# Adding the second half of an output in memory with GpSimd's transfers instead of on VectorE

## The chip, the cores and the metric

The kernel runs on one core of a Trainium2 chip. Its time is the device time of one execution in microseconds (us). Before the change three runs took 1242.47, 1244.1 and 1243.73 us; the median is 1243.73 us.

## The reference, cut to what matters

Three stages follow each other on 8 batches (`x` is 8 x 8 x 512 x 64, `state` 8 x 8 x 32 x 64):

```
xread, sread = state attention of x and state        # 8 x 544 rows, 512 columns
x   = (max(xa @ w_in, 0) ** 2) @ w_out               # 4352 rows; 512 -> 2048 -> 512
out = (((x @ w1) * (x @ w2)) @ w3) @ w_out2          # 512 -> 1024 -> 1024 -> 512, float32
```

Only the last line touches the change. The kernel multiplies `w3 @ w_out2` once into one 1024 x 512 matrix (`w34`), so that the last line is a product of 4352 x 1024 activations `c` with `w34`. The 1024 inner rows are summed in two halves of 512.

## The kernel before, in words

Every float32 product is made of three passes (high times high, low times high, high times low), so one logical product is three MATMUL instructions of 128 x 128 by 512 columns.

The 4352 output rows are nine pieces: `c` = 0 to 7 are the 512 token rows of each batch (four tiles of 128 rows each), and `c` = 8 (called `B` in the code) holds the 8 x 32 state rows (two tiles). So there are 34 output tiles of 128 x 512 float32, 256 KB each.

The last stage goes over all pieces twice, in two sweeps (loop at L952). Sweep `s` = 0 computes the first 512 columns of `c` and their part of the output, sweep 1 the other 512 columns and the rest of the output. Within a sweep the state piece comes first (`ab9`, then two output tiles), then four pairs of batches: (3,4), (5,6), (7,2), (0,1) in sweep 0 and the same in reverse in sweep 1. A pair is four calls of `quad` (42 matmuls each; L825 to L862) and then eight output tiles.

- `out_tile` (L904) is one output tile: 12 matmuls into a PSUM bank called `po` (tag `h`, two banks). In sweep 0 ScalarE copies the bank to an SBUF tile `o` (L916) and SyncE stores it to a scratch tensor `oscr` (L917). In sweep 1 VectorE adds the bank and the scratch tile that was loaded again (`opart`), into `o` (L919), and SyncE stores `o` into the output (L923, or L928 for the state rows, four stores of 32 rows a tile).
- `o` has the tag `yo` with two buffers: the tile after next can be written only when the transfer out of the buffer has landed.
- `load_o` (L899) loads `oscr` again. Its buffers are shared: `pt` with the loads of `load_pair` (L785), `s1` and `s2` with two of the temporaries that `quad` keeps (L836).
- `load_pair` (L778) loads the next pair's activations, 2 MB, on SyncE's queue; where a piece had been written in parts, the parts are added by GpSimd (L787). `make_pair` (L791) turns them into split tiles on ScalarE (L84) and VectorE (L85, L804) while the output tiles run.

The order on each engine is laid down by a scheduler when the kernel is built; the program's order is only its starting point. So the trace shows matmuls of the next pair's `quad` between output tiles.

Of the kernel before, what the change touches and what calls it, by code (L numbers as in the profile page):

```python
# [8 lines left out]
F32 = mybir.dt.float32  # L9
# [4 lines left out]
ALU = mybir.AluOpType  # L14
# [6 lines left out]
def kernel(  # L21
# [17 lines left out]
    nc = tc.nc  # L39
    B, H, S, D = x.shape  # L40
    NS = state.shape[2]
    DM = H * D
    DF = w_in.shape[1]
    D1 = w1.shape[1]
    T = S + NS
    P = 128
    G = 2
    HG = H // G
    J = S // P
# [9 lines left out]
    def f32(ap):  # L59
        return ap.bitcast(F32)  # L60
# [4 lines left out]
    dram = ctx.enter_context(tc.tile_pool(name="dram", bufs=1, space=DRAM))  # L65
# [8 lines left out]
    def bank_h(name):  # L74
        return psum.tile([P, 512], F32, tag="h", bufs=2, name=name)
# [476 lines left out]
    xp, sc, s2, s1a, s1b, at, a2t, sr, srt = att_steps(0)  # L552
# [74 lines left out]
    for b in range(BLK, B):  # L627
# [5 lines left out]
        for g in range(G):  # L633
            i = (b - 2) * NF + 12 + g
# [103 lines left out]
    bp = None  # L738

    def load_w(s):  # L740
        raw = []
        for kt in range(2):
            t = wpool.tile([P, 4, 512], F32, tag="wi1", bufs=2, name="wraw")
            for n, (i, k) in enumerate(((0, kt), (0, 2 + kt), (1, kt), (1, 2 + kt))):
                nc.sync.dma_start(t[:, n], w12_s[i][k][:, s, :])
            raw.append(t)
        return raw
# [30 lines left out]
    def load_pair(c0, c1):  # L778
        raw = []
        for kt in range(2):  # L780
            t = wpool.tile([P, 4, 512], F32, tag="wi1", bufs=2, name="yraw")
            for n, (c, d) in enumerate(((c0, kt), (c1, kt), (c0, 2 + kt), (c1, 2 + kt))):
                nc.sync.dma_start(t[:, n], y_scr[c][0][:, d, :])
                for part in y_scr[c][1:]:
                    p = bp.tile([P, 512], F32, tag="pt", bufs=2, name="yp")  # L785
                    nc.sync.dma_start(p, part[:, d, :])
                    nc.gpsimd.tensor_tensor(out=t[:, n], in0=t[:, n], in1=p, op=ALU.add)  # L787
            raw.append(t)
        return raw
# [35 lines left out]
    def quad(c0, c1, m):  # L825
        def product(ps, w, v, first=True, last=True):
            for kt in range(2):
                for k, (wi, vi) in enumerate(PASSES):
                    nc.tensor.matmul(  # L829
                        ps, W[w, kt][:, wi, m * P:(m + 1) * P], Y[v, kt][:, vi, :],  # L830
                        start=(first and kt == 0 and k == 0), stop=(last and kt == 1 and k == 2),
                        skip_group_check=True,
                    )

        def kept(i, ps):
            t = bp.tile([P, 512], F32, tag=f"s{i}", bufs=1 + (i == 0), name=f"s{i}")  # L836
            nc.scalar.copy(t, ps)  # L837
            return t

        def plus(t, ps):  # L840
            nc.vector.tensor_tensor(out=t, in0=ps, in1=t, op=ALU.add)  # L841

        A, D, E, C = bank_m("qa"), bank_y(m % 2, "qd"), bank_y(2, "qe"), bank_y(3, "qc")
        product(A, "A11", "B11", last=False)
        p1 = kept(0, A)
        product(D, "S1", "T1", last=False)
        p5 = kept(1, D)
        product(E, "A12", "B21")
        plus(p1, E)
        product(A, "S2", "T2", first=False, last=False)  # L850
        u2 = kept(2, A)
        product(D, "S4", "B22", first=False)
        plus(u2, D)
        product(C, "A22", "T4")
        product(A, "S3", "T3", first=False)
        u3 = kept(3, A)
        plus(p5, A)
        nc.vector.tensor_tensor(out=u2, in0=u2, in1=p5, op=ALU.mult)  # L858
        to_c(c1, m, u2, 512)
        plus(u3, C)  # L860
        nc.vector.tensor_tensor(out=p1, in0=p1, in1=u3, op=ALU.mult)
        return to_c(c0, m, p1, 512)  # L862
# [9 lines left out]
    def make9(raw):  # L872
        for d in range(ND):
            t = bp.tile([P, 2, 512], F32R, tag="c", bufs=2 * QM, name="y9q")
            split(t[:, HI, :NT9], t[:, LO, :NT9], raw[d // 2][:, d % 2])
            Y[B, d] = t

    def ab9(m):
        pss = [bank_y(2 * i + m % 2, "ab") for i in range(2)]
        for i in range(2):  # L880
            for d in range(ND):
                w = W[f"A{i + 1}{d // 2 + 1}", d % 2]
                for k, (wi, vi) in enumerate(PASSES):
                    nc.tensor.matmul(  # L884
                        pss[i][:, :NT9], w[:, wi, m * P:(m + 1) * P], Y[B, d][:, vi, :NT9],
                        start=(d == 0 and k == 0), stop=(d == ND - 1 and k == 2),
                    )
        a = bp.tile([P, 512], F32, tag="s0", bufs=2, name="a")
        nc.scalar.copy(a[:, :NT9], pss[0][:, :NT9])
        nc.vector.tensor_tensor(out=a[:, :NT9], in0=pss[1][:, :NT9], in1=a[:, :NT9], op=ALU.mult)  # L890
        to_c(B, m, a[:, :NT9], NT9)

    def n_out(c):
        return (512 if c < B else NT9) // P

    o_scr = {(c, t): dram.tile([P, DM], F32, name=f"oscr{c}_{t}") for c in range(B + 1) for t in range(n_out(c))}
    o_in = {}

    def load_o(c, t):  # L899
        tag = ("pt", "pt", "s1", "s2")[t]  # L900
        o_in[c, t] = bp.tile([P, DM], F32, tag=tag, bufs=2 if tag == "pt" else 1, name="opart")
        nc.sync.dma_start(o_in[c, t], o_scr[c, t])

    def out_tile(c, t, s):  # L904
        ps = bank_h("po")
        for m in range(QM):
            v, kk = c_t[c, m], s * QM + m
            w = w34_t[kk // 2][:, kk % 2]
            for k, (vi, wi) in enumerate(PASSES):
                nc.tensor.matmul(  # L910
                    ps, v[:, vi, t * P:(t + 1) * P], w[:, wi, :],
                    start=(m == 0 and k == 0), stop=(m == QM - 1 and k == 2),
                )
        o = pa.tile([P, DM], F32, tag="yo", bufs=2, name="o")
        if s == 0:
            nc.scalar.copy(o, ps)  # L916
            nc.sync.dma_start(o_scr[c, t], o)  # L917
            return
        nc.vector.tensor_tensor(out=o, in0=ps, in1=o_in.pop((c, t)), op=ALU.add)  # L919
        if c < B:  # L920
            rows_t = "(p j) e -> j p e" if c < BLK else "(j p) e -> j p e"
            dst = out[c * T:c * T + S, :].rearrange(rows_t, j=J)[t]
            nc.sync.dma_start(dst, o)  # L923
        else:
            nb = P // NS
            for i in range(nb):
                r0 = (t * nb + i) * T + S
                nc.sync.dma_start(out[r0:r0 + NS, :], o[i * NS:(i + 1) * NS, :])  # L928


    rows = list(range(N1 // 2, N1)) + list(range(N1 // 2))
# [13 lines left out]
    bp = ctx.enter_context(tc.tile_pool(name="bp", bufs=1, reuse_waits="tile"))  # L945
# [6 lines left out]
    for s, todo in enumerate((pairs, pairs[::-1])):  # L952
        if s == 1:
            make9(raw9)
            for t in range(n_out(B)):
                load_o(B, t)
        for m in range(QM):
            ab9(m)
        for t in range(n_out(B)):
            out_tile(B, t, s)  # L960
        for i, (c0, c1) in enumerate(todo):
            for m in range(QM):
                last = quad(c0, c1, m)
                if m == 0 and i + 1 < len(todo):
                    raw = load_pair(*todo[i + 1])
                if m == 1 and i + 1 == len(todo) and s == 0:
                    raw = load_w(1)
            outs = [(c, t) for c in (c0, c1) for t in range(n_out(c))]
            if s == 1:
                for o in outs[:3]:  # L970
                    load_o(*o)
            for n, (c, t) in enumerate(outs):
                if s == 1 and n + 3 < len(outs):
                    load_o(*outs[n + 3])
                out_tile(c, t, s)
                with tc.issue_after(last.ins):
                    if n == 0 and i + 1 < len(todo):
                        make_pair(raw)
                    if n == 0 and i + 1 == len(todo) and s == 0:
                        raw9 = load9()  # L980
                        make_w(raw)
            if s == 0 and i + 1 == len(todo):
                for j in range(N1 // 4):
                    w34_t[N1 // 4 + j] = wpool.tile([P, 2, 2, DM], F32R, tag="wi0", bufs=2, name="w34b")
                    nc.sync.dma_start(f32(w34_t[N1 // 4 + j]), w34_s[j])
# [29 lines left out]
```

## Time and profile before

| what | value |
| --- | --- |
| median of three runs | 1243.73 us |
| profiled execution, its own time | 1244.7 us |
| its span in the trace | 1242.7 us |
| granted TensorE clock, mean | 0.995 of full speed |
| TensorE busy | 1226.2 us (99%) |
| VectorE busy | 780.8 us (63%) |
| ScalarE busy | 623.9 us (50%) |
| GpSimd busy | 102.9 us (8%) |
| `oscr<-o` stores / `opart<-oscr` loads | 34 / 34, 256 KB each |

The profile names PE (TensorE's matmuls), PEld (its weight loads), DVE (VectorE), ACT (ScalarE), POOL (GpSimd) and SP (SyncE, which here only issues transfers; SPq is its queue). An engine works through its instructions in order. A bracket at the end of a timeline line gives the idle time before the instruction and what ended it. The busy time of PE is modelled, since matmuls are pipelined, so gains and losses on PE are better read from when the same point of the program is reached.

### The profile page before, as it was taken

To read this page: it belongs to the slowest core of one execution; us is meant where nothing else is said; L and a number is where in the kernel's file an instruction comes from. 1 tells how busy PE (TensorE), PEld (TensorE's weight loads), DVE (VectorE), ACT (ScalarE), POOL (GpSimd) and SP (SyncE) were. 2 spreads that over 40 slices of the span, in tenths; PEclk is the share of its full clock that TensorE was granted. 3 is DMA by queue.
4 is the path that set the end of the run, shared out by engine and by line. 5 is a ranking of instruction groups with operands and counts; after the bars stand their busy time and mean duration, and the time that the engine had idled before them with its cause. 6 is when DMAs were issued, how large, how long until landed. Compare 5 with 4: busy or idle time off the path is not lost.

```text
span 1242.7 us, 17483 instructions
## 1 busy us (share of the span) xinstructions
PE 1226.2 (99%) x6608; PEld 977.0 (79%) x6608; DVE 780.8 (63%) x1406; ACT 623.9 (50%) x1129; POOL 102.9 (8%) x158
## 2 busy tenths in 40 slices
PE   6999999999999999999999999999999999999998
PEld 4677777777777777777799888888888888887886
DVE  6987877677686766642346835555755548475753
ACT  6777556565464645545556534444443534333330
POOL 0000001232421101100000000102400010000000
PEclk9999999999999999999999999999999999999999
DMA  7354655744645363201423520404430522323213
GB/s 237 103 187 152 170 149 174 164 130 103 153 123 145 119 141 129 71 18 34 102 69 119 203 85 1 152 17 152 120 136 17 204 68 65 139 88 117 84 52 118
DMA packets 124179, 143.22 MB, mean 115 GB/s; under 512 B 72640, under 2 KB 76224, under 8 KB 123584
## 3 DMA queue, kind: packets, MB, share of 16 engines
q1 hardware_dynamic: 114368, 110.65, 29.6%
q0 software_dynamic: 9728, 31.47, 8.1%
q8 instruction: 51, 0.84, 0.3%
q14 instruction: 32, 0.26, 0.1%
HBM read 96.47 MB, written 45.61 MB: 114 GB/s over the span
## 4 chain that ended last, share of the span: by engine, by line
PE 94%; DMA 2%; DVE 2%; ACT 1%; SPq 1%; issue 0%; DVEq 0%
PE y L501 30%; PE po L910 13%; PE qa L829 10%; PE qd L829 7%; PE ps_w L714 4%; PE qc L829 3%; PE qe L829 3%; PE ps_sw L433 3%; PE ab L884 2%; DMA x<-in_x_dram 1%; PE ps_s L302 1%; DMA out_dram<-o 1%; DVE yq L85 1%; PE ps_r L379 1%; PE ps_a L371 1%; DMA st<-in_state_dram 0%
## 5 line engine op out<-in xcount | busy, mean ns | idle before, releaser
L501 PE MATMUL y<-ghl,wo 128*128 128x512 f32 (+1 forms) x1728 | 402.5, 381 | 0.3 <-ACT wo L84 0.2
L501 PEld LDWEIGHTS y<-ghl,wo 128*128 128x128 f32 x1728 | 309.3, 188 | 87.1 <-ACT r L449 15.1
L85 DVE TENSOR_TENSOR ghl<-r,ghl 128x512 fp32r<-128x512 f32 (+1 forms) x144 | 94.7, 658 | 161.3 <-ACT ghl L84 158.2
L829 PE MATMUL qa<-yq,wq 128*128 128x512 f32 x576 | 146.4, 390 | 0.8 <-ACT s L837 0.8
L837 ACT COPY s<-qa 128x512 f32<-128x512 f32 x96 | 56.2, 589 | 143.8 <-PE qa L829 131.2
L829 PEld LDWEIGHTS qa<-yq,wq 128*128 128x128 f32 x576 | 107.5, 188 | 24.8 <-ACT s L837 1.7
L829 PE MATMUL qd<-yq,wq 128*128 128x512 f32 x384 | 98.2, 390 | 0.0
L910 PE MATMUL po<-w34b,c 128*128 128x512 f32 x408 | 95.8, 391 | 0.3 <-DVE o L919 0.3
L910 PE MATMUL po<-w,c 128*128 128x512 f32 x408 | 95.4, 391 | 0.0
L910 PEld LDWEIGHTS po<-w34b,c 128*128 128x128 f32 x408 | 75.7, 188 | 18.0 <-DVE c L85 1.0
L451 ACT ACTIVATE r<-r 128x512 f32<-128x512 f32 (+1 forms) x144 | 87.8, 610 | 3.3
L910 PEld LDWEIGHTS po<-w,c 128*128 128x128 f32 x408 | 75.5, 188 | 17.7 <-ACT o L916 1.1
L84 ACT CAST ghl<-r 128x512 fp32r<-128x512 f32 (+1 forms) x144 | 86.2, 598 | 3.7
L829 PEld LDWEIGHTS qd<-yq,wq 128*128 128x128 f32 x384 | 71.8, 188 | 15.5 <-ACT s L837 0.8
L841 DVE TENSOR_TENSOR s<-qa,s 128x512 f32<-128x512 f32 x32 | 22.1, 692 | 74.5 <-ACT s L837 74.5
L787 POOL TENSOR_TENSOR yraw<-yraw,yp 128x512 f32<-128x512 f32 x24 | 32.2, 1345 | 436.2 <-DMA yraw<-yscr 305.8
L84 ACT CAST c<-s 128x512 fp32r<-128x512 f32 x64 | 39.7, 622 | 36.4 <-DVE s L858 35.4
L84 ACT CAST yq<-yraw 128x512 fp32r<-128x512 f32 x70 | 42.6, 623 | 21.4 <-DVE yraw L804 15.5
L919 DVE TENSOR_TENSOR o<-po,opart 128x512 f32<-128x512 f32 x34 | 23.3, 689 | 46.4 <-PE po L910 34.8
L85 DVE TENSOR_TENSOR c<-s,c 128x512 fp32r<-128x512 f32 x64 | 48.3, 773 | 2.1
L829 PE MATMUL qc<-yq,wq 128*128 128x512 f32 x192 | 49.5, 390 | 0.0
L829 PE MATMUL qe<-yq,wq 128*128 128x512 f32 x192 | 49.2, 389 | 0.0
(561 smaller groups left out, 1809.8 us busy)
## 6 DMA issues: line engine op xcount, KB each, us to landing
yraw<-yscr SPq DMA_DIRECT2D x56, 256.0 KB, 5.1
yscr<-yo SPq DMA_DIRECT2D x52, 256.0 KB, 2.7
oscr<-o SPq DMA_DIRECT2D x34, 256.0 KB, 2.0
opart<-oscr SPq DMA_DIRECT2D x34, 256.0 KB, 2.9
raw<-in_moe_w_out_dram SPq DMA_DIRECT2D x16, 512.0 KB, 4.6
raw<-in_moe_w_dram POOLq DMA_DIRECT2D x64, 128.0 KB, 3.4
raw<-in_moe_w_dram POOLq DMA_DIRECT2D x16, 512.0 KB, 4.3
out_dram<-o SPq DMA_DIRECT2D x32, 256.0 KB, 2.9
```

The costliest lines, as they stand in the source:

```text
L84: nc.scalar.copy(hi, src)
L85: return nc.vector.tensor_tensor(out=lo, in0=src, in1=f32(hi), op=ALU.subtract)
L433: mm = nc.tensor.matmul(pss[r][k * NS:(k + 1) * NS, cols], stT[rows, b, k, :], win_t[fg][rows, k, cols], start=True, stop=True, tile_posit ...
L451: nc.scalar.activation(r[:, :n], r[:, :n], ACTF.Square)
L501: nc.tensor.matmul(y_ps[c, d][:, :n], wo_t[f][:, wi, d * P:(d + 1) * P], t[:, gi, :n], start=(f == f0 and k == 0), stop=(f == f1 - 1 and k ...
L714: nc.tensor.matmul(ps, t[:, wi, (j % 4) * P:(j % 4 + 1) * P], wo2_t[j][:, vi, :], start=(j == 0 and k == 0), stop=(j == N1 - 1 and k == 2),)
L787: nc.gpsimd.tensor_tensor(out=t[:, n], in0=t[:, n], in1=p, op=ALU.add)
L829: nc.tensor.matmul(ps, W[w, kt][:, wi, m * P:(m + 1) * P], Y[v, kt][:, vi, :], start=(first and kt == 0 and k == 0), stop=(last and kt == ...
L837: nc.scalar.copy(t, ps)
L884: nc.tensor.matmul(pss[i][:, :NT9], w[:, wi, m * P:(m + 1) * P], Y[B, d][:, vi, :NT9], start=(d == 0 and k == 0), stop=(d == ND - 1 and k ...
L910: nc.tensor.matmul(ps, v[:, vi, t * P:(t + 1) * P], w[:, wi, :], start=(m == 0 and k == 0), stop=(m == QM - 1 and k == 2),)
L919: nc.vector.tensor_tensor(out=o, in0=ps, in1=o_in.pop((c, t)), op=ALU.add)
```

## The change

In both sweeps ScalarE now copies the PSUM bank to `o`. Sweep 0 stores `o` straight into the output, on SyncE's queue. Sweep 1 sends `o` to the same rows with a transfer that GpSimd issues and that adds to what is in memory (`accum_op=ALU.add`). The scratch tensor `oscr`, its 34 stores and 34 loads, and VectorE's 34 additions are gone. The state rows go out as four transfers a tile in both sweeps.

```diff
-    o_scr = {(c, t): dram.tile([P, DM], F32, name=f"oscr{c}_{t}") for c in range(B + 1) for t in range(n_out(c))}
-    o_in = {}
-
-    def load_o(c, t):
-        tag = ("pt", "pt", "s1", "s2")[t]
-        o_in[c, t] = bp.tile([P, DM], F32, tag=tag, bufs=2 if tag == "pt" else 1, name="opart")
-        nc.sync.dma_start(o_in[c, t], o_scr[c, t])
-
     def out_tile(c, t, s):
...
         o = pa.tile([P, DM], F32, tag="yo", bufs=2, name="o")
-        if s == 0:
-            nc.scalar.copy(o, ps)
-            nc.sync.dma_start(o_scr[c, t], o)
-            return
-        nc.vector.tensor_tensor(out=o, in0=ps, in1=o_in.pop((c, t)), op=ALU.add)
+        nc.scalar.copy(o, ps)
+
+        def put(dst, src):
+            if s == 0:
+                nc.sync.dma_start(dst, src)
+            else:
+                nc.gpsimd.dma_start(dst, src, accum_op=ALU.add)
+
         if c < B:
             rows_t = "(p j) e -> j p e" if c < BLK else "(j p) e -> j p e"
-            dst = out[c * T:c * T + S, :].rearrange(rows_t, j=J)[t]
-            nc.sync.dma_start(dst, o)
+            put(out[c * T:c * T + S, :].rearrange(rows_t, j=J)[t], o)
         else:
             nb = P // NS
             for i in range(nb):
                 r0 = (t * nb + i) * T + S
-                nc.sync.dma_start(out[r0:r0 + NS, :], o[i * NS:(i + 1) * NS, :])
+                put(out[r0:r0 + NS, :], o[i * NS:(i + 1) * NS, :])
...
         if s == 1:
             make9(raw9)
-            for t in range(n_out(B)):
-                load_o(B, t)
...
-            if s == 1:
-                for o in outs[:3]:
-                    load_o(*o)
             for n, (c, t) in enumerate(outs):
-                if s == 1 and n + 3 < len(outs):
-                    load_o(*outs[n + 3])
                 out_tile(c, t, s)
```

## Rows read from the trace of the kernel before

**Rows 1.** The page, busy time of each engine: us, share, instructions.

```profile
PE 1226.2 (99%) x6608; PEld 977.0 (79%) x6608; DVE 780.8 (63%) x1406; ACT 623.9 (50%) x1129; POOL 102.9 (8%) x158
```

**Rows 2.** Waits of PE, whole run: total us, times, longest.

```profile
PE qa L829 <- ACT s L837: 0.8, 1, 0.8
PE po L910 <- DVE o L919: 0.3, 1, 0.3
```

**Rows 3.** Timeline of PE, sweep 0: first output matmuls of each pair (start, length).

```profile
776.45 4.75 PE L910 MATMUL po<-w,c 128*128 128x512 f32 x20
...
836.44 4.75 PE L910 MATMUL po<-w,c 128*128 128x512 f32 x20
...
896.45 4.75 PE L910 MATMUL po<-w,c 128*128 128x512 f32 x20
...
956.50 4.75 PE L910 MATMUL po<-w,c 128*128 128x512 f32 x20
```

**Rows 4.** The same in sweep 1; the last two are the end.

```profile
1033.70 4.75 PE L910 MATMUL po<-w34b,c 128*128 128x512 f32 x20
...
1094.08 4.75 PE L910 MATMUL po<-w34b,c 128*128 128x512 f32 x20
...
1155.43 4.75 PE L910 MATMUL po<-w34b,c 128*128 128x512 f32 x20
...
1215.84 5.95 PE L910 MATMUL po<-w34b,c 128*128 128x512 f32 x24
1222.09 16.64 PE L910 MATMUL po<-w34b,c 128*128 128x512 f32 x72 [0.31 <-DVE o L919]
```

**Rows 5.** Timeline around the longest stall of PE in sweep 1.

```profile
1127.67 0.69 DVE L919 TENSOR_TENSOR o<-po,opart 128x512 f32<-128x512 f32 x1 [2.99 <-DMA out_dram<-o]
...
1128.40 0.59 ACT L837 COPY s<-qa 128x512 f32<-128x512 f32 x1 [3.09 <-DMA yraw<-yscr]
...
1129.04 1.66 PE L829 MATMUL qa<-yq,wq 128*128 128x512 f32 x6 [0.78 <-ACT s L837]
```

**Rows 6.** Timeline of one pair's output tiles in sweep 0.

```profile
841.95 1.08 ACT L916 COPY o<-po 128x512 f32<-128x512 f32 x2 [1.55 <-PE po L910]
842.56 9.69 SPq L917 DMA_DIRECT2D oscr<-o  x5
...
842.67 16.54 PE L910 MATMUL po<-w,c 128*128 128x512 f32 x72
...
845.69 0.59 ACT L916 COPY o<-po 128x512 f32<-128x512 f32 x1 [1.50 <-PE po L910]
```

**Rows 7.** Line 919: duration ns min/median/max, first and last start us; then its idle time.

```profile
L919 DVE TENSOR_TENSOR o<-po,opart x34: 678/691/692, 993.8 to 1238.8; 128x512 f32<-128x512 f32 x34
...
  DMA out_dram<-o: 11.6, 5
```

**Rows 8.** Line 916.

```profile
L916 ACT COPY o<-po x34: 579/588/593, 738.5 to 979.6; 128x512 f32<-128x512 f32 x34
```

**Rows 9.** Line 923, SyncE's stores into the output.

```profile
L923 SPq DMA_DIRECT2D out_dram<-o x32: 332/338/932, 1040.2 to 1239.5; - x32
...
DMA to landing us min/median/max: 2.0/2.9/5.3
```

**Rows 10.** Line 902, the loads of the partial outputs.

```profile
DMA to landing us min/median/max: 2.4/2.9/5.2
```

**Rows 11.** Line 221, GpSimd's stores of 256 KB, 40 in all.

```profile
L221 POOL DMA_DIRECT2D w3s<-cw x16: 549/587/591, 256.3 to 396.4; - x16
...
DMA to landing us min/median/max: 2.3/2.4/8.2
```

**Rows 12.** Timeline, all engines, where the sweeps meet.

```profile
980.17 0.32 SPq L917 DMA_DIRECT2D oscr<-o  x1
...
994.50 4.45 SPq L928 DMA_DIRECT2D out_dram<-o  x8
```

**Rows 13.** Windows: one pair of sweep 1 (us, busy by engine, clock, DMA share, GB/s).

```profile
1094.00:1155.40 61.40, 60.62 (x266) 48.97 (x265) 38.79 (x62) 21.80 (x38) 0.00 (x0) 1.00 0.31 103
```

## The prediction

> **What bounds the kernel now.** I read the page first, then PE's waits, then the timelines of the two sweeps side by side. The page says that TensorE is busy 99% of the span, VectorE 63%, ScalarE 50% and GpSimd 8% [rows 1]. So work taken off VectorE is worth nothing in itself; it is worth what TensorE waits for it. The waits of PE put only two in the part that the change touches: 0.78 us for a copy of ScalarE and 0.31 us for VectorE's addition [rows 2]. They understate it, since small delays of weight loads are not counted as idle. The timelines give the whole: from the first output matmul of one pair to that of the next, sweep 0 takes 836.44 - 776.45 = 59.99, then 60.01 and 60.05 us [rows 3]; sweep 1, with the same 264 matmuls, 60.38, 61.35 and 60.41 us [rows 4]. Sweep 0 evicts its output tiles with ScalarE and has no loads of partial outputs. So all that sweep 1 pays for the VectorE form is (60.38 + 61.35 + 60.41) - (59.99 + 60.01 + 60.05) = 2.09 us, plus the 0.31 us in the last pair [rows 4]. That is the most that the trace lets me expect on TensorE, 0.2% of the time.
>
> **Where the 2.09 us come from.** The largest piece can be followed [rows 5]: VectorE's addition at 1127.67 waited 2.99 us for an earlier store out of the same `o` buffer. It ended at 1128.36, and at 1128.40 ScalarE's copy of the next `quad` began, although the row puts its wait down to a transfer. That copy writes a temporary whose buffer `opart` had occupied until the addition read it; 0.04 us after the addition is the release. TensorE then stood 0.78 us. VectorE waited for such stores five times, 11.6 us in all [rows 7].
>
> **Part by part.**
>
> *The loads and VectorE's additions go; ScalarE's copies come.* VectorE loses 34 x 0.691 = 23.5 us [rows 7], ScalarE gains 34 x 0.588 = 20.0 us [rows 8]. Per pair ScalarE goes from 21.80 to 21.80 + 8 x 0.59 = 26.5 us of a 61.4 us stretch, VectorE from 38.79 to 33.3 us [rows 13]; neither is near its limit. With `opart` gone, the `quad` temporaries wait for no output tile. Sweep 1 then has the instruction list of sweep 0, and I take sweep 0's pace for it: -2.1 us for the three pairs, -0.3 us in the last. Bounds: the full -2.4 on one side; on the other 0, if the scheduler lays the matmuls out in a way that loses as much elsewhere.
>
> *Sweep 0 stores into the output instead of the scratch.* 32 stores stay what they were in size and number. The state piece's two become eight of 64 KB, which take SyncE 4.45 us to issue where sweep 1 does it now [rows 12], against 2 x 0.32. What follows them in the queue are loads for the next pair, wanted some 40 us later. Cost 0, and up to 1 us if `o`'s buffer is held longer.
>
> *Sweep 1's transfers move to GpSimd's queue.* GpSimd needs 0.55 to 0.59 us to issue one [rows 11], against 0.34 on SyncE [rows 9]; per pair eight of them are 4.7 us, where GpSimd is idle (0.00 us busy) [rows 13]. So the issue is not the limit; the landing may be, because it frees `o`.
>
> *When does a slow landing reach TensorE?* Take sweep 0's pair [rows 6]. Eight tiles, with two `o` buffers and two banks; the last six are 72 matmuls in 16.54 us, which less the last one's run-out is 2.72 us a tile. The first transfer is issued at 842.56 and ScalarE's third copy wants its buffer at 845.69, 3.13 us later. The copy may be late, though, until TensorE wants the bank for the fifth tile: the last 72 matmuls are tiles three to eight, so tile five starts at 842.67 + 2 x 2.72 = 848.11. With 0.6 us of copying and 0.1 us of signalling, the copy must start by 847.4. So a landing of L = 4.85 us costs nothing. The same bound holds for the steady pace: two tiles take 2 x 2.72 = 5.44 us, the copy 0.59, which leaves 4.85. Beyond it TensorE loses, by stepping through the eight tiles, about 1.2 us a pair at L = 5.5, 2.3 at 6 and 5 at 7.
>
> *What is L?* The trace has no adding transfer. Below it lies GpSimd's plain store of 256 KB, 2.3 us at the least and 2.4 at the median [rows 11]. Above it I put a store with a whole load in front, since the memory must be read before it is written: 2.3 + 2.4 (the least of the `opart` loads [rows 10]) = 4.7 us. On a quiet queue both ends are under 4.85: no cost. Beside the 2 MB loads of a next pair, which fall on the output tiles of the first two pairs of sweep 1, plain stores took up to 5.3 us [rows 9]; with a load in front that is 7.7 us. But GpSimd's transfers won't stand behind those loads in SyncE's queue as the stores do now. I take L = 4 quiet and 5.0 loaded: 0.3 us for each of two pairs, 0.6 in sum (bounds 0 and about 2 x 7 = 14).
>
> The Trainium skill ("DMA: Bandwidth & Descriptors", section "Anatomy of one DMA") gives GpSimd's path a fixed 2.0 us plus the bytes over 436e3 per us, an estimate of 2.6 us for 256 KB; the trace's median of 2.4 is somewhat below. Counting the bytes twice for the read the page would give an estimate of 3.2 us, and no stall anywhere.
>
> *The tail.* TensorE's last matmul ends at 1222.09 + 16.64 = 1238.73 [rows 4], VectorE adds for 0.69, and the last store is issued at 1239.5 [rows 9]; the span ends at 1242.7, 3.97 us after that matmul. After: a copy of 0.59 (-0.1 us), and a transfer of between 2.3 and 4.7 us where the store took 2.0: +0.3 to +2.7 us. I take +1.5, the middle, because neither end is the nearer row. This is wholly on the path.
>
> **The sum.** -2.1 - 0.3 + 0.6 - 0.1 + 1.5 = -0.4 us. The profiled execution took 1244.7 us (span 1242.7, 2.0 around it); after the change it would be 1244.3. It lies 0.97 us above the median of the three runs, so for the median 1243.73 - 0.4 = 1243.3 us. A measurement of this kernel cannot tell less than 0.2%, 2.5 us, from no change, and this is far inside.
>
> **The rivals.**
>
> *The landing becomes the bound (slower).* If the adding transfer needs 6 to 7 us, ScalarE's copies wait for `o`, the `po` banks stay full and TensorE stands in all four pairs. The point from which it decides is L = 4.85 us. For it: only two buffers, and five waits of this very kind already with plain stores [rows 7]. Against: the quiet bounds lie under 4.85. Price at L = 6.5: about 3.5 us in each of three pairs and 3 in the last, its tail 4.4 longer than now: 10.5 + 3 + 4.4 - 2.5 = +15, 1259 us.
>
> *The adding transfers wait for one another (slower).* The Trainium skill (same page, "Rules for kernel authors") says that an accumulating transfer must wait for the semaphore of an earlier access to the same bytes; no run here shows one yet. For the same rows that costs nothing: the last store of sweep 0 is issued at 980.17 [rows 12], the first of sweep 1's 32 at 1040.2 [rows 9]. But if the ordering is kept for the output as a whole, or for the interleaved rows of batches 0 to 2, each waits for the one before. Then a tile takes L + 0.1 = 4.1 us or more instead of 2.72, five of eight tiles pay 1.4 us: 7 us a pair, 28 in all, 1270 us. Against: today's stores to the same tensor are issued 0.56 us apart (eight in 4.45 us [rows 12]), each before the one in front has landed.
>
> *It gains more.* The adding transfer costs little more than a store (tail +0.3) and the freed temporaries let the pairs run without even sweep 0's slack (264 matmuls at 2.72 / 12 us are 59.84, 0.15 to 0.2 us under its 60.0): -2.4 - 0.1 + 0.3 - 0.6 = -2.8 us, 1240.9. Against: it needs both.
>
> **How the numbers follow.** The forecast has 0.62, and of that 0.55 lies within 2.5 us of before (0.03 below, 0.04 above). The landing as the bound has 0.22, nearly all slower; the chain of waits 0.05; more gain 0.11, 0.10 of it below. So faster 0.13, same 0.57, slower 0.30. The forecast's own range is 1241.0 (no stall, tail +0.3) to 1246 (no gain on TensorE, tail +2.7). I widen it to 1250 for landings of up to some 6 us, and leave out 1259 and 1270.
>
> **What would show it.** Right: the pairs of sweep 1 at 60.0 us, no wait of PE above 0.5 us at `po`, the adding transfers' landing under 4.85 us at the median, the span ending 4 to 6.6 us after the last matmul. Wrong: ScalarE's copies waiting for `DMA out_dram<-o` at every tile and PE for those copies, pairs over 62 us, or GpSimd's issues waiting for a transfer instead of for ScalarE.

## The result, and the profile after

The changed kernel is slower. In the first comparison it took 1253.99 us (median of four runs) against 1243.47 us; the ratio is 1.0088, 95% interval [1.0067, 1.0109]. The forecast of 1243.3 us and its range up to 1250 us were wrong. The profiled execution took 1252.45 us, with a span of 1250.5 us, 7.8 us more than before.

The page's busy times: TensorE does the same 6608 matmuls, VectorE has lost 34 additions, ScalarE has gained 34 copies, GpSimd 40 transfers [rows 1].

```profile
PE 1225.0 (98%) x6608; PEld 976.9 (78%) x6608; DVE 758.1 (61%) x1372; ACT 641.9 (51%) x1163; POOL 137.0 (11%) x198
```

The timeline of PE in sweep 1 answers to [rows 4]: the first output matmuls of each pair, the last 72 matmuls, and the two stalls (start, length, in brackets the idle time).

```profile
1031.83 4.75 PE L902 MATMUL po<-w34b,c 128*128 128x512 f32 x20
...
1061.53 1.66 PE L829 MATMUL qa<-yq,wq 128*128 128x512 f32 x6 [3.23 <-ACT s L837]
...
1095.67 4.75 PE L902 MATMUL po<-w34b,c 128*128 128x512 f32 x20
...
1124.18 2.63 PE L829 MATMUL qa<-yq,wq 128*128 128x512 f32 x6 [2.35 <-ACT s L837]
...
1159.93 4.75 PE L902 MATMUL po<-w34b,c 128*128 128x512 f32 x20
...
1219.95 5.94 PE L902 MATMUL po<-w34b,c 128*128 128x512 f32 x24
1226.10 16.63 PE L902 MATMUL po<-w34b,c 128*128 128x512 f32 x72 [0.21 <-ACT o L907]
```

The account, from these rows and [rows 4]:

| part | before, us | after, us | difference |
| --- | --- | --- | --- |
| start to the first pair's output tiles in sweep 1 | 1033.70 | 1031.83 | -1.87 |
| pair (0,1) to (7,2) | 60.38 | 63.84 | +3.46 |
| pair (7,2) to (5,6) | 61.35 | 64.26 | +2.91 |
| pair (5,6) to (3,4) | 60.41 | 60.02 | -0.39 |
| last eight tiles | 22.89 | 22.78 | -0.11 |
| last matmul to end | 3.97 | 7.77 | +3.80 |
| span | 1242.7 | 1250.5 | +7.8 |

Of the first line, -2.71 us stand there before the change does anything: the first output tile of all came at 732.89 here against 735.60, that of sweep 0's first pair at 773.74 against 776.45 (between 774.28 and 776.00 in the runs below). From that pair to the first pair of sweep 1 the changed kernel took 258.09 us against 257.25, 0.84 us more, in sweep 0 and the state tiles behind it.

The timeline where the first stall arises (all engines):

```profile
1050.35 5.20 SPq L783 DMA_DIRECT2D yraw<-yscr  x8
...
1051.29 0.87 POOL L913 DMA_DIRECT2D out_dram<-o  x1 [1.56 <-ACT o L907]
...
1060.41 0.58 ACT L907 COPY o<-po 128x512 f32<-128x512 f32 x1 [6.24 <-DMA out_dram<-o]
1060.89 0.59 ACT L837 COPY s<-qa 128x512 f32<-128x512 f32 x1
```

SyncE issues the eight loads of the next pair within 5.2 us. The adding transfer of the sixth tile is issued among them, at 1051.29. The copy of the eighth tile needs its `o` buffer and starts at 1060.41, 9.1 us later, after ScalarE has sat idle for 6.24 us. The next `quad`'s copy stands behind it on ScalarE, and TensorE needs that one to reuse the `qa` bank: 3.23 us of standing. The matmuls of the output tiles, where the prediction had put the cost, were hardly held back: the last 72 of the pair took 16.86 us against 16.54 [rows 6]. So 3.23 of the 3.84 us that this pair lost against 60.0 are the stall.

The lines of the adding transfers, for the whole run, and then their landing in the third pair alone, where no load runs (min/median/max us). They answer to [rows 9] and [rows 11].

```profile
L913 POOL DMA_DIRECT2D out_dram<-o x40: 842/855/2816, 996.4 to 1243.7; - x40
...
DMA to landing us min/median/max: 2.5/4.0/9.0
```

```profile
DMA to landing us min/median/max: 3.7/4.0/5.2
```

### The profile page after: what moved, and what is told of

It is laid out like the page before. It is cut to its first block, busy times and chain, and to the rows that moved or that the text cites. A ratio compares the mean times of both kernels' runs of the same rounds, so it can differ in the third digit from the quotient of the medians.

```text
span 1250.5 us, 17419 instructions
## 1 busy us (share of the span) xinstructions
PE 1225.0 (98%) x6608; PEld 976.9 (78%) x6608; DVE 758.1 (61%) x1372; ACT 641.9 (51%) x1163; POOL 137.0 (11%) x198
## 4 chain that ended last, share of the span: by engine, by line
PE 74%; issue 17%; POOL 2%; DMA 2%; DVE 2%; ACT 1%; SPq 0%; POOLq 0%; ACTq 0%
PE y L501 30%; PE po L902 6%; PE qa L829 5%; PE ps_w L714 3%; PE qd L829 3%; PE ps_sw L433 3%; POOL out_dram L913 2%; PE ab L884 2%; PE qc L829 2%; PE qe L829 2%; DMA x<-in_x_dram 1%; DVE yq L85 1%; PE ps_s L302 1%; DMA wraw<-w12s 1%; PE ps_r L379 1%
## 5 line engine op out<-in xcount | busy, mean ns | idle before, releaser
L907 ACT COPY o<-po 128x512 f32<-128x512 f32 x68 | 39.1, 587 | 83.5 <-PE po L902 48.6
L787 POOL TENSOR_TENSOR yraw<-yraw,yp 128x512 f32<-128x512 f32 x24 | 34.8, 1450 | 423.4 <-DMA yraw<-yscr 403.8
L841 DVE TENSOR_TENSOR s<-qe,s 128x512 f32<-128x512 f32 x32 | 22.1, 690 | 70.6 <-PE qe L829 50.0
L913 POOL DMA_DIRECT2D out_dram<-o x40 | 33.8, 1079 | 215.2 <-ACT o L907 213.0
L841 DVE TENSOR_TENSOR s<-qd,s 128x512 f32<-128x512 f32 x32 | 22.1, 691 | 50.6 <-PE qd L829 47.6
```

The costliest lines, as they stand in the source:

```text
L913: nc.gpsimd.dma_start(dst, src, accum_op=ALU.add)
```

## The experiments

All times are medians against the kernel before in the same comparison: 1244.31 us for e1 to e4, 1244.7 us for e5 to e8 (times of the two groups are best compared by their ratios). "Pairs" are the three intervals of the table; "end" is from the last matmul to the end of the span. For scale, the changed kernel again:

**e8: the changed kernel once more.** No edit.

> The changed kernel once more, on the chip of the others, for a time to compare them with: 1252 to 1256 us, pairs of sweep 1 near 64, 64 and 60 us, the end 7.8 us after the last matmul.

Measured: 1256.6 us, ratio 1.0099 [1.0085, 1.0112]; pairs 65.56, 66.72 and 60.01, end 7.61 us. The stalls were a little longer, 3.70 and 3.53 us, and matmuls behind them ran longer (in the last section).

**e1: GpSimd stores without adding.**

```diff
-                nc.gpsimd.dma_start(dst, src, accum_op=ALU.add)
+                nc.gpsimd.dma_start(dst, src)
```

> Leaves out the addition: in sweep 1 GpSimd's transfers only store, so the output holds the second half alone. The order of instructions on every engine is that of the changed kernel. Two theories of why the transfers beside the eight loads landed after 9.0 us. (A) It is the addition: the memory's row is read before it is written, and that read stands in the queue of the loads. Then a plain store lands as SyncE's do: about 2.4 us quiet and at most 5.3 loaded, no stall of TensorE over 0.5 us, pairs of sweep 1 at 60.0 us (63.84 and 64.26 in the changed kernel), the end about 6 us after the last matmul (7.8), and a time near 1244 us. (B) It is the burst: SyncE now issues the eight loads in 5 us, and whatever GpSimd sends meanwhile waits for the DMA engines. Then a plain store lands after 7 to 9 us beside the loads, both stalls stay (2 to 3 us each), and the time stays within 3 us of the changed kernel's, 1251 to 1254 us.

Measured: 1244.05 us, ratio 0.9998 [0.9989, 1.0007]. Pairs 60.00, 60.02 and 60.00, end 6.16 us. The lines of its transfers, and PE in sweep 1:

```profile
L913 POOL DMA_DIRECT2D out_dram<-o x40: 496/539/566, 999.1 to 1236.9; - x40
...
DMA to landing us min/median/max: 1.9/2.3/6.5
```

```profile
1033.16 4.75 PE L902 MATMUL po<-w34b,c 128*128 128x512 f32 x20
...
1093.16 4.75 PE L902 MATMUL po<-w34b,c 128*128 128x512 f32 x20
...
1153.18 4.75 PE L902 MATMUL po<-w34b,c 128*128 128x512 f32 x20
...
1213.18 5.93 PE L902 MATMUL po<-w34b,c 128*128 128x512 f32 x24
1219.33 16.61 PE L902 MATMUL po<-w34b,c 128*128 128x512 f32 x72 [0.21 <-ACT o L907]
```

Theory A is right in the main: without the addition the same order of instructions, with the same burst of loads (4.43 us here), has no stall. But the burst is not innocent: a plain store landed after up to 6.5 us beside the loads, more than A's 5.3. That is late enough for two copies to wait 3.5 us each, and not late enough for TensorE. The issue also became shorter, 0.54 us instead of 0.85; that this is not what cured the stalls shows e3, where the issue takes 0.85 us and no such stall is left.

**e2: four buffers for the adding transfers.**

```diff
...
-        o = pa.tile([P, DM], F32, tag="yo", bufs=2, name="o")
+        turn = len(outs_done) % 2
+        outs_done.append((c, t))
+        if s == 1 and turn:
+            o = bp.tile([P, DM], F32, tag="pt", bufs=2, name="o")
+        else:
+            o = pa.tile([P, DM], F32, tag="yo", bufs=2, name="o")
```

> In sweep 1 every second output tile gets its buffer from the pool of the part loads, so four buffers instead of two; order on TensorE, ScalarE and VectorE unchanged. If the stalls come from the buffer alone (a copy of ScalarE waits for the transfer of two tiles before, and the next quad's copies stand behind it): landings stay at 9 us beside the loads, but no copy waits for a transfer for over 1 us, both stalls go, pairs of sweep 1 at 60.0 to 60.5 us; the tail of 7.8 us stays; time near 1247 us. Rival: the transfers hold TensorE back in another way (the loads of the next pair late, matmuls at a lower clock): pairs stay above 62 us, time above 1250 us.

Measured: 1244.83 us, ratio 1.0006 [0.9997, 1.0015]; pairs 59.99, 60.00 and 60.03, end 7.74 us. The landing of its transfers:

```profile
DMA to landing us min/median/max: 2.6/4.2/10.2
```

The transfers are as late as ever, 10.2 us at the most, and no copy of `o` waits for an adding transfer any more. So the chain from the landing to TensorE goes through the two `o` buffers. It came out 2 us below the 1247 expected, because I had subtracted from a changed kernel that I took to be 1254 us with the profiled run's stalls; against e8, by the ratios, the difference is 0.93%, 11.6 us.

**e3: no loads beside the adding transfers.** Two buffers; the loads wait on SyncE's queue for a small store of the last tile.

```diff
...
+                if s == 1 and n + 1 == len(outs):
+                    mark.append(nc.sync.dma_start(mark_scr, o[:, :128]))
...
-                    raw = load_pair(*todo[i + 1])
+                    with tc.issue_after(mark[-1].ins) if mark else nullcontext():
+                        raw = load_pair(*todo[i + 1])
```

> The addition stays, with two buffers; but in sweep 1 the loads of the next pair are held on SyncE's queue behind a small store of the last output tile (64 KB to scratch, for the order only), so that no load runs beside the adding transfers. If the burst of loads is what makes them late: all landings between 3.7 and 5.2 us as in the quiet pairs, no stall over 0.5 us, pairs at 60.0 us, tail 7.8, time near 1247 us. If the adding transfers were late by themselves (their own queue, GpSimd's issue of 0.85 us), landings of 9 us and the stalls stay: 1251 to 1254 us. If the held loads come too late for the next pair, TensorE waits for ScalarE's or VectorE's splits some 45 us after the last tile.

Measured: 1245.9 us, ratio 1.0015 [1.0007, 1.0024]; pairs 60.62, 59.99 and 59.99, end 7.85 us. The landing in its first pair, and the one delay of PE there:

```profile
DMA to landing us min/median/max: 4.0/4.9/7.1
```

```profile
1038.38 5.64 PE L905 MATMUL po<-w34b,c 128*128 128x512 f32 x24
1038.54 1.77 POOL L916 DMA_DIRECT2D out_dram<-o  x2 [33.19 <-ACT o L910]
1043.69 0.58 ACT L910 COPY o<-po 128x512 f32<-128x512 f32 x1 [3.80 <-DMA out_dram<-o]
1044.33 11.19 PE L905 MATMUL po<-w34b,c 128*128 128x512 f32 x48 [0.31 <-ACT o L910]
```

The 7.1 us belong to the last tile's transfer, which was issued at 1056.99, just ahead of the held loads, and whose buffer nobody wants soon. The first transfer was issued at 1038.54 and its buffer was written again at 1043.69, 5.15 us later; the pair lost 0.62 us. The way that the prediction worked out, through the bank of the fifth tile, is there, but its limit of 4.85 us is some 0.3 us too high: SyncE had issued 0.11 us before the third tile's first matmul [rows 6], GpSimd here 0.16 us after it. The first pair of the changed kernel agrees (third tile from 1038.05, issue at 1038.22):

```profile
1038.05 16.86 PE L902 MATMUL po<-w34b,c 128*128 128x512 f32 x72
1038.22 1.77 POOL L913 DMA_DIRECT2D out_dram<-o  x2 [34.16 <-ACT o L907]
...
1043.07 0.59 ACT L907 COPY o<-po 128x512 f32<-128x512 f32 x1 [3.49 <-DMA out_dram<-o]
```

There the buffer was written again 4.85 us after the issue, and the 72 matmuls took 0.32 us longer than in [rows 6]. A limit of 4.6 us would give 0.25 and 0.55 us, near both losses. What a pair pays when all its landings are late, no run shows.

**e4: SyncE stores without adding**, the floor.

```diff
-                nc.gpsimd.dma_start(dst, src, accum_op=ALU.add)
+                nc.sync.dma_start(dst, src)
```

> Leaves out the addition: sweep 1 stores plainly, on SyncE's queue, as sweep 0 does. Order on TensorE, VectorE and ScalarE as in the changed kernel. This is the floor of what taking the additions off VectorE can give. My forecast's first term says pairs at 60.0 us against 60.38, 61.35 and 60.41 before, and an end some 4 us after the last matmul: 2.4 us less than before, near 1241 us. Rival: SyncE's stores stand behind the burst of loads and land after 7 us or more, so that the stalls come back without GpSimd: pairs above 61 us, time above 1243 us.

Measured: 1240.54 us, ratio 0.997 [0.9959, 0.9981]; pairs 60.00, 60.02 and 60.02. The last matmuls and the line of its stores:

```profile
1219.66 16.64 PE L902 MATMUL po<-w34b,c 128*128 128x512 f32 x72 [0.21 <-ACT o L907]
```

```profile
L913 SPq DMA_DIRECT2D out_dram<-o x40: 315/332/425, 994.4 to 1237.0; - x40
...
DMA to landing us min/median/max: 1.7/2.0/6.3
```

The end is 1239.9 - 1236.30 = 3.6 us. This confirms the forecast's first term: VectorE's additions and the second loads cost the three pairs 2.1 us, and taking them away gives that back. The profiled span is 2.8 us shorter than before: 2.1 in the pairs, 0.1 in the last tiles, 0.4 at the end, 0.2 ahead of sweep 1's pairs. The medians differ by 3.8 us; where the other 1.0 lies is not shown.

**e5 and e6: the last tile, or the last two, the old way**, with four buffers for the rest.

```diff
...
+            if s == 1 and i + 1 == len(todo):
+                for n, (c, t) in enumerate(outs[-2:]):     # e5: outs[-1:]
+                    o_in[c, t] = bp.tile([P, DM], F32, tag=f"s{n + 1}", bufs=1, name="opart")
+                    nc.sync.dma_start(o_in[c, t], rows_of(c, t))
...
+        if (c, t) in o_in:
+            nc.vector.tensor_tensor(out=o, in0=ps, in1=o_in[c, t], op=ALU.add)
+            nc.sync.dma_start(rows_of(c, t), o)
+            return
```

> Four buffers as before, and the very last output tile done the old way (its first half loaded from the output, VectorE's addition, SyncE's store). The end of the program came 7.74 us after the last matmul with an adding transfer, 6.16 with GpSimd's plain store and 3.6 with SyncE's. Theory: of the 4 us lost, about 1.6 are the addition and about 2 are a fixed time between the landing of GpSimd's last transfer and the end of the program. Then GpSimd's last transfer, now of the tile before, is issued 2.7 us earlier and still ends the program: 7.74 - 2.72 = 5.0 us after the last matmul. Without such a fixed time it would be hidden: 4.0 us, as in the kernel before. Pairs at 60.0 us either way; time near 1242 us.

> Four buffers, and the last two output tiles done the old way. By either theory GpSimd's last transfer is now early enough: the end 3.6 to 4.0 us after the last matmul, pairs at 60.0 us, about 3.8 us less than with four buffers alone: near 1241 us against 1244.3 before, that is faster than both kernels. Rival: the four buffers and the loads leave something else late in the last pair (the loads of the halves, VectorE's addition), and the time stays at 1244 us or above.

Measured: e5 1242.73 us, ratio 0.9985 [0.9976, 0.9994], end 5.08 us; e6 1241.56 us, ratio 0.9976 [0.9966, 0.9986], end 4.0 us; pairs 60.0 us in both. The last transfers of e5 (its span is 1240.7 us, its last matmul ends at 1235.62):

```profile
1233.87 0.86 POOL L929 DMA_DIRECT2D out_dram<-o  x1 [1.85 <-ACT o L923]
...
1236.43 0.34 SPq L921 DMA_DIRECT2D out_dram<-o  x1
```

SyncE's store of the very last tile landed 2.3 us after 1236.43, at 1238.7. GpSimd's, issued 2.56 us before it, took 4.1 us and landed at 1238.0, and the program ended at 1240.7. From GpSimd's last landing to the end it was 2.7 us here, 2.7 in the changed kernel (1243.7 + 4.1 to 1250.5) and 2.9 in e1 (1236.9 + 2.3 to 1242.1); from SyncE's it was 0.9 us in e4 (1237.0 + 2.0 to 1239.9) and 1.2 in the kernel before. So the longer time goes with GpSimd's queue; what it consists of stays open. With one tile more between (e6) it is hidden. e6 is faster than both kernels, by 0.24% against the one before.

**e7: the loads let go two at a time.** Two buffers.

```diff
...
+                if s == 1:
+                    mark.append(nc.sync.dma_start(mark_scr[n], o[:16, :128]))
...
+                with tc.issue_after(gates[4 + (4 * kt + n) // 2].ins) if gates else nullcontext():
+                    nc.sync.dma_start(t[:, n], y_scr[c][0][:, d, :])
```

> The changed kernel with its two buffers; in sweep 1 the eight loads are let go two at a time, each two behind a small store (8 KB to scratch, for the order only) of the output tiles five to eight. The kernel before had its loads spread like this, since its stores stood between them on SyncE's queue. If what hurts is that they come in one burst of 5 us: landings up to 6.5 us, no stall of TensorE over 1 us, pairs of sweep 1 at 60 to 61 us, time near 1246 us. If it is enough that loads run beside the adding transfers at all: landings of 8 to 9 us and stalls of 2 to 3 us stay, time 1251 us or more.

Measured: 1252.83 us, ratio 1.0063 [1.005, 1.0077]; pairs 62.04, 64.85 and 60.00. In the first pair (all engines; issues of the loads, the transfer of the sixth tile, the copy that waits for it, the stall):

```profile
1051.33 0.34 SPq L784 DMA_DIRECT2D yraw<-yscr  x1
...
1052.60 0.88 POOL L917 DMA_DIRECT2D out_dram<-o  x1 [1.73 <-ACT o L911]
1052.69 1.37 SPq L784 DMA_DIRECT2D yraw<-yscr  x3
...
1060.06 0.58 ACT L911 COPY o<-po 128x512 f32<-128x512 f32 x1 [4.39 <-DMA out_dram<-o]
...
1061.18 1.66 PE L830 MATMUL qa<-yq,wq 128*128 128x512 f32 x6 [1.73 <-ACT s L838]
```

The second theory held on the whole: the loads now spread over 10.8 us (11.6 before the change), and the transfer's buffer still came free only after 7.5 us; another transfer landed after 8.8. TensorE stood 1.73 us here and 2.95 in the second pair. So the loads' presence is enough. What the burst adds is less clear: the first pair lost less than in the changed kernel (62.04 against 63.84 us), the second more (64.85 against 64.26). My idea that the kernel before had been saved by its spread loads fell with this run.

**Why the adding transfer suffers more than a store.** The queue view gives for a window the packets, the MB, and the time that the packets took as a share of the time of all 16 DMA engines. First the eight adding transfers of the third pair of the changed kernel, then the eight plain ones of the third pair of e1, on the same queue, each in 26 us without loads (from 1164 to 1190 and from 1157.5 to 1183.5):

```profile
q0 software_dynamic: 1152, 2.10, 60.9%
```

```profile
q0 software_dynamic: 640, 2.10, 21.4%
```

One adding transfer of 256 KB took 0.609 x 26 / 8 = 1.98 us of all engines, a plain one 0.214 x 26 / 8 = 0.70 us: the addition took 2.8 times the packet time. Beside the loads of the first pair the engines were then about as busy in both kernels, and moved less with the addition (the last three numbers are the granted clock, the DMA share and GB/s; the changed kernel, then e1):

```profile
1051.00:1060.00 9.00, 7.30 (x33) 5.71 (x31) 0.10 (x1) 0.58 (x1) 1.73 (x2) 1.00 0.87 204
```

```profile
1051.00:1060.00 9.00, 9.00 (x41) 7.48 (x40) 0.84 (x2) 2.30 (x5) 1.62 (x3) 1.00 0.91 291
```

That fits a price paid in the time of the DMA engines, but it is a reading and not shown: times of packets can overlap (a share of 1.10 stands in the last section). How the engines divide themselves between the two queues no run here shows either.

## Why the prediction was wrong, step by step

- *What bounds the kernel, and what sweep 1 pays for VectorE's form.* Right. 60.38, 61.35 and 60.41 us were taken to become sweep 0's 60.0: the undisturbed pair of the changed kernel took 60.02, all nine of e1, e2 and e4 59.99 to 60.03.
- *Sweep 0's stores into the output.* Cost 0 taken, up to 1 us allowed: 0.84 us in the profile of the changed kernel, nothing in e8 (257.22 us from sweep 0's first pair to sweep 1's, against 257.25 before).
- *The limit of 4.85 us.* The mechanism was right, the limit some 0.3 us too high for GpSimd's later issue: 4.85 us cost 0.32 us in the changed kernel and 5.15 us cost 0.62 in e3.
- *What L is, quiet.* Right at the median, 4.0 taken and 4.0 measured. The upper bound of 4.7 was too low: single landings without loads beside them took 5.2 us in the third pair and up to 5.7 in e3's first pair. The estimate of 3.2 us by the page "DMA: Bandwidth & Descriptors" of the Trainium skill lay below, and the measurement decides.
- *What L is beside the loads.* This step failed. I took 5.0 us, with bounds to 7.7, on the ground that "GpSimd's transfers won't stand behind those loads in SyncE's queue". They landed after up to 9.0 us, beyond the bound. Three things were missed. A sign of it stood in [rows 11], of which I used the least and the median and passed over the greatest: a plain store of GpSimd had landed after 8.2 us in the kernel before. It was issued at 311.94, beside a load of SyncE's that landed after 10.3 us and loads of GpSimd's own. Leaving SyncE's queue does not leave the DMA engines: the Trainium skill ("DMA: Bandwidth & Descriptors", section "Issuing engines are not separate DMA queues") says that transfers from all engines run on the same 16 DMA engines and interleave, and the trace agrees, 4.0 us quiet against 9.0 beside the loads. And the price of an addition was put down as latency (a load in front of a store) and not as time of the DMA engines too, which the packet times suggest (2.8 times). That it takes both, the addition and the loads, is shown by e1 and e3. The term of 0.6 us was measured as 3.84 + 4.26 = 8.1 us above the 60.0 us pace, and 12.3 us in e8.
- *Where it reaches TensorE.* Half right: the two `o` buffers are the link, as e2 shows. But the large waits, 3.23 and 2.35 us, went on through ScalarE's order of instructions to the next `quad`; through the `po` banks went only the 0.32 us of the first pair.
- *The tail.* Mis-sized: +1.5 us taken, bounds +0.3 to +2.7, measured +3.8. Against e4's 3.6 us the end is 4.2 us longer. GpSimd's plain store (e1, 6.16) accounts for 2.6 of them, the addition for the other 1.6. The missing part is a time after the landing of GpSimd's last transfer, which no row of before could show, because GpSimd issued its last transfer there at 541.8 us.
- *The rival that came true* is the first, the landing as the bound, with 0.22. It decided in the two pairs with loads only, not in all four as I had priced it.
- *The transfers waiting for one another* did not happen: the third pair ran at 60.02 us, and each issue waited for ScalarE.

## What to carry to other kernels

A transfer that adds in memory is no free addition: it moves work from an engine with room to the DMA engines, where it took 2.8 times the packet time of a plain store here, and its landing beside a bulk load sets how many source buffers are needed. Before moving a transfer to another queue, look at what else runs on the DMA engines in the same stretch, and follow each late landing to the instruction that stands behind it in order. Look for the queue after which the program ends soonest and give it the last transfers; here the last two tiles the old way and four buffers for the rest turned a loss of 0.9% into a gain of 0.24%.

## What the runs showed of the hardware that was not expected

A stall may cost more than itself. The granted clock in four stretches behind the second stall of the changed kernel (window, its length, busy times of PE, PEld, DVE, ACT and POOL, clock, DMA share, GB/s):

```profile
1120.00:1124.00 4.00, 1.83 (x9) 1.17 (x7) 0.00 (x0) 0.95 (x2) 0.07 (x1) 1.00 1.10 278
1124.00:1126.00 2.00, 1.82 (x5) 1.49 (x6) 0.69 (x1) 0.62 (x2) 0.79 (x1) 0.64 1.07 339
1126.00:1128.00 2.00, 2.00 (x6) 1.52 (x6) 0.00 (x0) 0.59 (x1) 0.00 (x0) 0.51 0.65 124
1128.00:1130.00 2.00, 2.00 (x10) 1.62 (x9) 0.69 (x1) 0.00 (x0) 0.00 (x0) 1.00 0.00 0
```

TensorE had stood for 2.35 us; then the clock lay at about half of full speed, 1.2 instead of 2.4 GHz, and twelve matmuls took 4.45 us (1124.18 to 1128.63) instead of 2.72. In e8 it lasted longer behind the second stall, of 3.53 us:

```profile
1127.00:1130.00 3.00, 2.42 (x6) 1.94 (x7) 0.69 (x1) 1.02 (x3) 0.85 (x1) 0.50 0.95 242
1130.00:1133.00 3.00, 3.00 (x9) 2.32 (x8) 0.00 (x0) 0.59 (x1) 0.00 (x0) 0.50 0.25 32
```

There 18 matmuls took 7.10 us instead of 4.08. Behind e8's first stall, of 3.70 us, 12 matmuls took 4.40 us, and behind e7's second, of 2.95 us, the clock fell to 0.50 as well. The first stall of the changed kernel, 3.23 us, had no such sequel, nor had e7's first, 1.73 us; the clock stayed at 1.00. In the two pairs of the changed kernel the stalls come to 5.6 us and the slow matmuls to 1.7, of the 8.1 lost against sweep 0's pace; in e8 to 7.2 and 4.7, of 12.3. When the clock falls behind a stall, and when not, stays open.
